# One weight remainder issued on ScalarE's queue, one small copy moved to VectorE, in the first microseconds of a fused attention and SwiGLU kernel

## The chip, the cores and the metric

The kernel runs on one core of a Trainium2 chip. The metric is device time in microseconds (us) of one execution, and a kernel's time is the median of several executions. One execution was also recorded by the hardware profiler; its rows give the start and the length of each instruction on each engine: PE (TensorE's matmuls), PEld (TensorE's weight loads), DVE (VectorE), ACT (ScalarE), POOL (GpSimd) and SP (SyncE, which here only issues DMAs). A name with a q behind it (SPq, ACTq) is the engine's instruction queue, where it issues a DMA. L145 means line 145 of the kernel file.

## The reference

One token block x of 2048 rows by 576 columns (bf16) is normalised, and two branches run on the normalised rows; their sum is added to x.

```python
xn = layernorm(x)                       # no scale, no shift
# branch A: 32 heads of 18, window of 8 keys, dilation 2, causal
q, k, v = split(xn @ wqkv)              # wqkv: 576 x 1728
o = softmax(mask(q . k[pos - 2w] * 18**-0.5), over w = 0..7) . v[pos - 2w]
# branch B: SwiGLU
h = silu(xn @ w_gate) * (xn @ w_up)     # 576 x 4608 each
out = x + o @ wo + h @ w_down           # wo: 576 x 576, w_down: 4608 x 576
```

## The kernel before

The 2048 tokens lie as 128 partitions by 16 rows: partition p holds tokens 16p to 16p+15, and "row r" is the set of 128 tokens with the same place r. The sum over the 576 columns is cut into five K tiles: four of 128, and a remainder of 64. The program is written as one straight order by hand; each engine works through its own instructions in that order, and waits are semaphores that a framework inserts. Each DMA takes the next of eight completion semaphores in turn, in program order over all queues, and waits until the DMA that had it before has landed.

The work has two stages. In the first, for each of the 16 rows, the row is normalised (VectorE, with the square root on ScalarE), turned so that K lies on partitions, and multiplied with the QKV weight on TensorE; ScalarE takes the products out of PSUM into Q, K and V. In the second stage, four groups of four rows run the SwiGLU branch in nine chunks each, with the attention of VectorE alongside, and the down and output projections at the end of each group.

The change lies in the first nine microseconds, before row 0 is multiplied. The names and lines:

- `load_x` (L145) loads one row of x for rows 0 to 3; L164 loads the other twelve in three chunks of four rows (4,608 bytes a partition).
- `load_w` (L149) loads K tile kt = 0 to 3 of the QKV weight, 128 partitions of 3,456 bytes. For kt = 4 (L152) it loads the remainder in two halves: the 64 weight rows for the first 864 output columns go to partitions 0 to 63, and the same 64 rows for the other 864 columns go to partitions 64 to 127. Each half has 64 runs of 1,728 bytes, 110.6 KB.
- The issue order before: ScalarE's queue takes row 0 of x and weight tile 1; SP's takes row 1 of x, weight tiles 0, 2, 3, the two remainder halves, rows 2 and 3 of x, and the three chunks. `load_gu` (L180 to L183) follows on SP with the first gate and up weights.
- `warm_pe` (L172, L175) keeps TensorE busy on constants until row 0 has come.
- Row 0 is treated in a way of its own: `ln_stats` (L212, L214) and `ln_sqrt` (L224, on ScalarE) work out mean and deviation; `ln_center` (L242, L244) only subtracts the mean, so that the row can be turned before the deviation is known; `transp_pe` (L250) turns it in five TensorE transposes, the first into PSUM tile `pa` and the other four into `pb`; `copy_pt` (L256) copies the turned tiles to SBUF, in three pieces: kt 0, kt 1 and 2, kt 3 and 4. The scale is applied when the products are taken out (L354, L356).
- `p_row0` calls `p_mm` (L289): for kt 0 to 3 four matmuls each, one for each group of 432 output columns; behind kt 2 the five transposes of row 1 and their copies (`first`); then four matmuls on the remainder. Groups 0 and 1 read the half on partitions 0 to 63, groups 2 and 3 the half on 64 to 127; the order is group 0, 2, 1, 3.
- Between, VectorE works on row 1 (statistics, reciprocal L229, scaling L235 and L237), whose turned form `p_row(1)` reads next.

Of the kernel before, what the change touches and what calls it, by code (L numbers as in the profile page):

```python
# [17 lines left out]
P = 128  # L18
H, DH, W, DIL = 32, 18, 8, 2
D = H * DH  # L20
HALF = D // 2
G = 432
# [48 lines left out]
def kernel(  # L71
# [11 lines left out]
    nc = tc.nc  # L83
# [6 lines left out]
    x_v = A_x.rearrange("b (p r) d -> p (b r) d", r=R)  # L90
# [33 lines left out]
    xc_b = [wdf[:, i * XC:(i + 1) * XC].rearrange("p (r d) -> p r d", d=D) for i in range(4)]  # L124
# [5 lines left out]
    wqkvr = hTf[:, 12 * D:12 * D + 2 * G]  # L130
# [13 lines left out]
    def load_x(eng, j):  # L144
        eng.dma_start(xc_b[0][:, j:j + 1, :], x_v[:, j:j + 1, :])  # L145

    def load_w(eng, kt):
        if kt < 4:
            eng.dma_start(wqkv[:, kt, :], A_wqkv[kt * P:(kt + 1) * P, :])  # L149
        else:  # L150
            for i in range(2):
                eng.dma_start(wqkvr[64 * i:64 * i + 64, :], A_wqkv[4 * P:D, 2 * G * i:2 * G * (i + 1)])  # L152

    load_x(nc.scalar, 0)
    load_x(nc.sync, 1)
    load_w(nc.scalar, 1)
    load_w(nc.sync, 0)
    make_identity(nc, ident[:])
    for kt in range(2, KT):
        load_w(nc.sync, kt)  # L160
    load_x(nc.sync, 2)
    load_x(nc.sync, 3)
    for c in range(1, 4):
        nc.sync.dma_start(xc_b[c], x_v[:, 4 * c:4 * c + 4, :])  # L164
    nc.scalar.activation(warm[:], eps_t[:], ACT.Sqrt)

    wp = ps.tile([P, 512], f32, name="warm_ps", tag="ps")
# [53 lines left out]
    def ln_sqrt(r, n=1):  # L221
        c, j = divmod(r, 4)
        xc, xn, mv, rstd = ln[c]
        nc.scalar.activation(rstd[:, j:j + n], mv[:, j:j + n, 1], ACT.Sqrt, bias=eps_t[:], scale=1.0)  # L224
# [14 lines left out]
    def ln_center(r, lo=0, hi=D):  # L239
        c, j = divmod(r, 4)  # L240
        xc, xn, mv, rstd = ln[c]
        nc.vector.tensor_scalar(xn[:, j, lo:hi], xc[:, j, lo:hi], mv[:, j, 0:1], None, op0=ALU.subtract)  # L242
        if hi == D:
            nc.vector.tensor_copy(xn[:, j, D:DPAD], xn[:, j, 512:D])  # L244

    def transp_pe(r, kts, pt):
        c, j = divmod(r, 4)
        xn = ln[c][1]
        for i, kt in enumerate(kts):
            nc.tensor.transpose(pt[:, i * P:(i + 1) * P], xn[:, j, kt * P:(kt + 1) * P], ident[:])  # L250

    def xT_of(r):
        return xcT if r == 0 else xnT[:, :, r * P:(r + 1) * P]

    def copy_pt(eng, r, kts, pt):
        eng(xT_of(r)[:, kts[0]:kts[-1] + 1, :],  # L256
            pt[:, 0:len(kts) * P].rearrange("p (k t) -> p k t", t=P))

    def new_pt():
        return ps.tile([P, 8 * P], bf16, name="pt", tag="ps")  # L260
# [213 lines left out]
    ln_stats(0)  # L474
    ln_center(0, 0, P)
    ln_sqrt(0)
    pa, pb = new_pt(), new_pt()
    transp_pe(0, (0,), pa)
    ln_center(0, P, D)
    transp_pe(0, range(1, KT), pb)  # L480
    copy_pt(nc.scalar.copy, 0, (0,), pa)
    copy_pt(nc.scalar.copy, 0, (1, 2), pb)
    ln_recip(0)
    ln_stats(1)
# [205 lines left out]
```

## Time and profile before

| | us |
|---|---|
| median of 3 runs (503.4 to 503.75) | 503.6 |
| the profiled execution, whole | 503.67 |
| its span, first to last instruction | 501.9 |
| TensorE busy in the span | 497.4 (99%) |
| VectorE busy | 329.1 (66%) |
| ScalarE busy | 200.9 (40%) |
| granted TensorE clock, mean | 1.000 |

The busy time of an engine is the time with an instruction under way, as a sum; the ends of matmuls are modelled, so a busy TensorE need not be at its peak rate. The view of the chain that ended last starts at the last instruction and goes back at each step to whatever released it; what lies on that chain sets the end, and what doesn't has slack. The timeline lists instructions by start, with the idle time of the engine before an instruction and what ended that idle time in brackets. The DMA view of a window lists packets, bytes and, by queue, the time of its packets as a share of 16 engines; q1 is the queue that SP issues on, q10 the one that ScalarE issues on.

### The profile page before, as it was taken

What the parts mean: (1) busy time and instruction counts of PE and PEld (TensorE: products, weight loads), DVE (VectorE), ACT (ScalarE), POOL (GpSimd) and SP (SyncE); (2) the same over time, 40 slices, a digit from 0 to 9 for tenths busy, and PEclk for the clock granted to TensorE, in tenths of its full rate; (3) what the DMA queues carried; (4) which work ended last, traced back from release to release, by engine and by line L of the source; (5) the groups of instructions that cost most, each with busy time, mean ns of one, the idle gap of its engine ahead of it and who ended that gap; (6) DMA issues with size and microseconds to landing.
All of it is one profiled execution on the core that took longest, in us unless ns stands there. A gap on an engine that the chain in (4) does not pass through costs nothing.

```text
span 501.9 us, 13272 instructions
## 1 busy us (share of the span) xinstructions
PE 497.4 (99%) x5799; PEld 282.9 (56%) x5799; DVE 329.1 (66%) x480; ACT 200.9 (40%) x417; POOL 0.7 (0%) x6
## 2 busy tenths in 40 slices
PE   8999999999999999999999999999999999999997
PEld 4555544444677644444777544445777444446775
DVE  5888598898999698999898139995980222221001
ACT  4756657645400255554300445557000454553000
POOL 0000000000000000000000000000000000000000
PEclk9999999999999999999999999999999999999999
DMA  8699999789922046637730154465600335552100
GB/s 311 175 192 241 305 285 315 230 266 310 232 88 61 25 133 199 185 108 226 139 103 33 29 184 141 144 188 158 136 25 14 104 105 183 149 183 39 28 14 25
DMA packets 77186, 75.42 MB, mean 150 GB/s; under 512 B 22708, under 2 KB 72528, under 8 KB 77128
## 3 DMA queue, kind: packets, MB, share of 16 engines
q1 hardware_dynamic: 76840, 73.98, 51.3%
q8 instruction: 45, 0.74, 0.6%
q10 hardware_dynamic: 288, 0.59, 0.3%
q14 instruction: 13, 0.11, 0.1%
HBM read 58.76 MB, written 5.90 MB: 129 GB/s over the span
## 4 chain that ended last, share of the span: by engine, by line
PE 98%; DMA 1%; SPq 0%; DVE 0%; issue 0%
PE g_ps L575 56%; PE d_ps L604 32%; PE qkv_ps L289 10%; DMA hT<-in_A_wqkv_dram 1%; SPq L149 0%; DVE ot L618 0%; PE pt L271 0%; SPq L145 0%
## 5 line engine op out<-in xcount | busy, mean ns | idle before, releaser
L575 PE MATMUL g_ps<-xnT,gu 64*128 64x512 bf16 x2592 | 280.4, 376 | 0.0
L575 PEld LDWEIGHTS <-gu 64*128 64x128 bf16 x2592 | 126.2, 94 | 152.9
L586 ACT ACTIVATE sg<-g_ps 128x512 bf16<-128x512 f32 x144 | 87.4, 607 | 156.6 <-PE g_ps L575 156.5
L604 PE MATMUL d_ps<-wd,hT 64*128 64x288 bf16 x2304 | 146.3, 283 | 0.0
L604 PEld LDWEIGHTS <-hT 64*128 64x128 bf16 x2304 | 112.0, 94 | 29.8
L588 DVE TENSOR_TENSOR hT<-sg,uc 128x512 bf16<-128x512 bf16 x144 | 60.2, 419 | 93.3 <-ACT uc L587 93.1
L587 ACT CAST uc<-g_ps 128x512 bf16<-128x512 f32 x144 | 85.5, 594 | 0.0
L403 DVE TENSOR_REDUCE PP<-PP 128x64 f32<-128x1152 bf16 x64 | 84.9, 1346 | 0.4
L289 PE MATMUL qkv_ps<-hT,xnT 64*128 64x432 bf16 x540 | 49.9, 342 | 0.0
L398 DVE TENSOR_TENSOR PP<-QO,Kr 128x2304 bf16<-128x2304 bf16 (+1 forms) x35 | 43.5, 1250 | 7.9 <-DMA Kr<-hT 7.6
L616 DVE TENSOR_TENSOR ot<-d_ps,xr 128x288 bf16<-128x288 f32 x30 | 12.3, 451 | 51.0 <-PE d_ps L604 51.0
L430 DVE TENSOR_TENSOR PP<-Vr,A 128x2304 bf16<-128x2304 bf16 (+1 forms) x35 | 43.3, 1251 | 0.4
L289 PEld LDWEIGHTS <-xnT 64*128 64x128 bf16 x540 | 26.1, 94 | 22.5 <-ACT xnT L275 0.2
L435 DVE TENSOR_TENSOR PP<-PP 128x2304 bf16<-128x2304 bf16 x24 | 32.5, 1354 | 0.3
L586 ACT ACT_TABLE_LOAD x5 | 6.4, 1283 | 47.2 <-PE g_ps L575 47.2
L604 PE MATMUL d_ps<-wo,xnT 64*128 64x288 bf16 x288 | 22.9, 283 | 0.0
L352 ACT CAST hT<-qkv_ps 128x288 bf16<-128x288 f32 (+2 forms) x60 | 21.9, 426 | 0.6 <-DMA Vr<-hT 0.3
L423 ACT ACTIVATE PP<-PP 128x1024 f32<-128x1024 f32 x4 | 4.2, 1056 | 31.2 <-DVE PP L419 31.2
L604 PEld LDWEIGHTS <-xnT 64*128 64x128 bf16 x288 | 14.0, 94 | 3.6
L618 ACT CAST ot<-d_ps 128x288 bf16<-128x288 f32 x1 | 0.4, 398 | 38.8 <-PE d_ps L604 38.8
L352 ACT CAST QO<-qkv_ps 128x432 bf16<-128x432 f32 (+1 forms) x30 | 12.3, 410 | 7.7 <-PE qkv_ps L289 7.7
L212 DVE BATCH_NORM_STATS2 stats<-wd 128x6 f32<-128x288 bf16 x32 | 12.9, 441 | 3.3 <-DMA wd<-in_A_x_dram 3.3
(50 smaller groups left out, 88.0 us busy)
## 6 DMA issues: line engine op xcount, KB each, us to landing
gu<-in_B_w_gate_dram SPq DMA_DIRECT2D x36, 512.0 KB, 4.0
gu<-in_B_w_up_dram SPq DMA_DIRECT2D x36, 512.0 KB, 5.3
wd<-in_B_w_down_dram SPq DMA_DIRECT2D x9, 576.0 KB, 6.3
kv_d<-hT SPq DMA_DIRECT2D x5, 576.0 KB, 5.9
gu<-in_B_w_gate_dram SPq DMA_DIRECT2D x36, 64.0 KB, 5.1
gu<-in_B_w_up_dram SPq DMA_DIRECT2D x36, 64.0 KB, 4.7
xr<-in_A_x_dram SPq DMA_DIRECT2D x8, 288.0 KB, 4.6
out_dram<-ot SPq DMA_DIRECT2D x16, 144.0 KB, 1.8
```

The costliest lines, as they stand in the source:

```text
L212: nc.vector.bn_stats(sums[r][:, k, :], xc[:, j, k * HALF:(k + 1) * HALF])
L289: return nc.tensor.matmul(t[g][:, 0:G], xT_of(r)[rows, kt, :], w_at(g, kt, rows), start=start, stop=stop)
L352: nc.scalar.copy(*parts[n])
L398: nc.vector.tensor_tensor(prod[:, a:b], QO[:, RT * tt + a:RT * tt + b, :], Kr[:, s:s + b - a, :], op=ALU.mult)
L403: nc.vector.tensor_reduce(L[:, w, rs], prod[:, rs].rearrange("p r (h d) -> p r h d", d=DH), axis=AX.X, op=ALU.add)
L430: nc.vector.tensor_tensor(dst[:, a:b], Vr[:, s:s + b - a, :].rearrange("p r (d h) -> p r d h", h=H), A[:, w, a:b].unsqueeze(2).to_broadcas ...
L435: nc.vector.tensor_tensor(dst, acc, pv, op=ALU.add)
L575: mm = nc.tensor.matmul(ring_ps[j][b][:], gu[rows, slot, k, fc], xnT[rows, kt, tok], start=(swap == 0 and kt == 0), stop=(swap == 1 and kt ...
L586: nc.scalar.activation(sg[:], t[0][:], ACT.Silu)
L587: nc.scalar.copy(uc[:], t[1][:])
L588: nc.vector.tensor_tensor(hT[:, ch * FC + j, :], sg[:], uc[:], op=ALU.mult)
L604: mm = nc.tensor.matmul(t[sub][h][:, 0:HALF], a[rows], w[rows, h * HALF:(h + 1) * HALF], start=(swap == 0 and n == 0), stop=(swap == 1 and ...
```

## The change

Two things are moved. The half of the remainder for partitions 64 to 127 is no longer issued on SP behind the first half, but on ScalarE's queue, in the program's order behind the square root of row 0. The loads of rows 2 and 3 of x and of the three chunks stay on SP in their order; in the program they now stand behind that place, so that the order in which DMAs take the eight semaphores is as before. And the copy of row 0's first turned tile (kt 0, 128 by 128) is done by VectorE instead of ScalarE; it stands on VectorE behind the 64-column copy of L244 and ahead of the reciprocal of L229. The number of instructions on TensorE and their order are as before.

```diff
@@ load_w
         else:
-            for i in range(2):
-                eng.dma_start(wqkvr[64 * i:64 * i + 64, :], A_wqkv[4 * P:D, 2 * G * i:2 * G * (i + 1)])
+            load_rem(eng, 0)
+
+    def load_rem(eng, i):
+        eng.dma_start(wqkvr[64 * i:64 * i + 64, :], A_wqkv[4 * P:D, 2 * G * i:2 * G * (i + 1)])
...
     for kt in range(2, KT):
         load_w(nc.sync, kt)
-    load_x(nc.sync, 2)
-    load_x(nc.sync, 3)
-    for c in range(1, 4):
-        nc.sync.dma_start(xc_b[c], x_v[:, 4 * c:4 * c + 4, :])
...
     ln_stats(0)
     ln_center(0, 0, P)
     ln_sqrt(0)
+    load_rem(nc.scalar, 1)
+    load_x(nc.sync, 2)
+    load_x(nc.sync, 3)
+    for c in range(1, 4):
+        nc.sync.dma_start(xc_b[c], x_v[:, 4 * c:4 * c + 4, :])
     pa, pb = new_pt(), new_pt()
     transp_pe(0, (0,), pa)
     ln_center(0, P, D)
     transp_pe(0, range(1, KT), pb)
-    copy_pt(nc.scalar.copy, 0, (0,), pa)
+    copy_pt(nc.vector.tensor_copy, 0, (0,), pa)
     copy_pt(nc.scalar.copy, 0, (1, 2), pb)
```

## The prediction

> **What bounds the kernel now.** I read three views in this order: the chain that ended last over the first 16 us, the VectorE, ScalarE and TensorE rows of the timeline around the edit, and the traffic of the DMA queues in short windows there. The chain first, cut to the stretch in question (start, length, what):
>
> ```profile
> 1.65 0.43 SPq L149
> 2.08 0.04 issue
> 2.12 6.78 DMA hT<-in_A_wqkv_dram
> 8.90 0.04 issue
> 8.94 3.73 PE qkv_ps L289 x34
> ```
>
> The end is set by one transfer: the fourth full weight tile (kt 3), issued on SP at 2.12 us, landed at 8.90. From 8.94 TensorE runs without a wait up to the tail. The windows show it: busy 18.06 of 18.06 us from 8.94 to 27, 33.00 of 33.00 up to 60, 438.00 of 438.00 up to 498. So whatever the edit does counts only by how it moves 8.94, or by a new wait behind it. All waits of TensorE in the whole span are three:
>
> ```profile
> PE warm_ps L172 <- PEq L674: 0.8, 1, 0.8
> PE pt L250 <- DVE wd L242: 0.3, 1, 0.3
> PE qkv_ps L289 <- DMA hT<-in_A_wqkv_dram: 0.2, 1, 0.2
> ```
>
> The last, 0.24 us, is the only one that a better weight stream could remove. A gain of 0.2% would be 1.0 us (about what a measurement of this kernel can tell from no change); the row bounds a gain there by 0.24.
>
> The rows around the edit (start, length, engine, line, what):
>
> ```profile
> 5.16 0.29 ACT L224 ACTIVATE rstd<-mv,eps_t 128x1 f32<-128x1 f32 x1 [2.00 <-DVE mv L214]
> 5.47 0.69 PE L250 MATMUL pt<-ident,wd 128*128 128x128 bf16 x5 [0.33 <-DVE wd L242]
> 5.70 0.18 DVE L244 COPY wd<-wd 128x64 bf16<-128x64 bf16 x1
> 5.74 0.27 ACT L256 COPY PP<-pt 128x128 bf16<-128x128 bf16 x1 [0.29 <-PE pt L250]
> 5.79 0.16 DVE L229 RECIPROCAL rstd<-rstd 128x1 f32<-128x1 f32 x1
> ...
> 6.06 2.36 PE L289 MATMUL qkv_ps<-hT,PP 128*128 128x432 bf16 x12
> 6.20 0.37 ACT L256 COPY PP<-pt 128x256 bf16<-128x256 bf16 x1 [0.20 <-PE pt L250]
> ...
> 8.26 0.44 PE L250 MATMUL pt<-ident,wd 128*128 128x128 bf16 x5
> 8.94 1.36 PE L289 MATMUL qkv_ps<-hT,PP 128*128 128x432 bf16 x8 [0.24 <-DMA hT<-in_A_wqkv_dram]
> ```
>
> The reader is to see that ScalarE copies the first turned tile at 5.74, that TensorE starts on it at 6.06, works to 8.70 and then stands still until 8.94. The matmuls on the remainder are the last four of the eight at 8.94; they start at 9.76, and the second of them, about 9.85, is the first to read partitions 64 to 127.
>
> The queues from 7.8 to 8.9 us, and then from 6.2 to 7.2 us:
>
> ```profile
> DMA packets 222, 0.25 MB, mean 228 GB/s; under 512 B 33, under 2 KB 222, under 8 KB 222
> ```
> ```profile
> DMA packets 137, 0.42 MB, mean 420 GB/s; under 512 B 15, under 2 KB 16, under 8 KB 137
> ```
>
> All engines are busy in both (104% and 103% of 16 engines). In the first no packet reaches 2 KB, so no row of a full weight tile (3,456 B) is left there; the last such packets are at 7.7, and the tile lands 1.2 us after them.
>
> **Part one: the second remainder leaves SP.** SP issued the two remainders from 2.60 to 3.94 us (0.70 and 0.60 us); they landed 6.7 and 6.3 us after issue, at 9.3 and 9.6, ahead of 9.76 and 9.85. Taking 0.60 us off SP gives nothing: SP's next issue, row 2 of x, starts at 4.05, just as the first row of x has landed (0.74 + 3.3): the program has it wait for that transfer's completion semaphore, which it takes over, and the order in which semaphores are taken over is unchanged. SP only waits longer there. The three chunks of x at 6.33 to 7.3 and the first gate and up weights at 8.92 wait for weight tiles in the same way (waits of up to 1.3 us each on the queue's own view). Sum 0.
>
> **Part two: ScalarE issues it.** It now stands behind the square root that ends at 5.45. Its price on the engine is between 0.41 us (ScalarE's own issues at 0.74 and 1.18 took 0.41 and 0.45) and 0.70 (SP's for this shape). I take 0.65, the same shape, so ScalarE is free at 6.10, and at the dear end at 6.15. Queued behind it is the copy of tiles 1 and 2, which starts at 6.20 for want of its transposes. Its reader, the fifth matmul, comes at 6.06 plus four times 0.18 (twelve in about 2.2 us), 6.78, and the copy ends at 6.57: 0.21 us more of cover. Cost 0; beyond 0.26 us of delay it would count first against the 0.24 of standstill.
>
> **Part three: the first copy moves to VectorE.** The trace has no such copy. Bounds are 0.18 us (64 columns on VectorE, L244) and 0.27 (this copy on ScalarE); the nearest row is VectorE's 256 columns from the same kind of bank, 0.24. I take 0.20. It follows the 64-column copy, where the reciprocal started at 5.79, and ends near 5.99, against 6.01 before: the first matmul moves by -0.05 to +0.1, I take 0. VectorE's later work slips by 0.17 (between 0.09, the spacing of the neighbouring rows, and 0.27): statistics and square root of row 1, its scaling, and so the five transposes at 8.26, which end at 8.87 instead of 8.70. The standstill covers that, with 0.07 left; at 0.27 it would cost 0.03. The turned row 1 is copied by 9.71 instead of 9.54, and read from 10.14. Cost 0.
>
> **Part four: the stream of weights.** The remainder's packets now come on ScalarE's queue. The first packets after x's issues at 0.74 came at 1.7 (SP) and 2.0 (ScalarE), 1.0 to 1.3 us; so here from 6.45 to 6.75, in the middle of the fourth tile, whose packets run from about 6.35 to 7.7. Before, they stood behind it. Do two queues share? Between 4.0 and 5.5 us:
>
> ```profile
> q10 hardware_dynamic: 104, 0.33, 54.3%
> q1 hardware_dynamic: 102, 0.30, 49.0%
> ```
>
> They do, packet by packet nearly equal. So the 64 packets, 110.6 KB, go between those of the fourth tile, and it ends later by at most their own service. Bounds: 0 (they come too late, or the tile's wait is in its completion and not in its packets; below nothing by 0.07, since the transposes end at 8.87) and 0.49 us (110.6 KB at the 228 GB/s of the remainders). The nearest row is the 420 GB/s of the stretch in which they arrive: 0.26. I take 0.26, since 6.75 leaves about 0.9 us of the tile's packets, and at half of 420 GB/s the 64 packets need 0.53. The first remainder lands 0.4 us behind the tile as before, at 9.56, needed at 10.0. The second lands, by the nearest row (x's first row on this queue, 3.3 us from issue to landing), at 8.75, needed at 10.1. Later work has no cost: row 2 of x, which VectorE awaited for 0.40 us at 9.94, comes no later than before.
>
> A rule speaks against any gain here: the Trainium skill, DMA: Bandwidth & Descriptors, section Issuing engines are not separate DMA queues, has all queues end on the same 16 engines, so that a second one saves only issue time; by that alone the sum would be 0, and the half shares above agree with it.
>
> **The sum.** 0 + 0 + 0 + 0.26 us on 503.67 (the profiled execution's own time; its span is 501.9, with 1.77 around it) is 503.93. That execution lies 0.07 above the median of 503.6 and inside the runs shown.
>
> **Rivals.** The second is that the fourth tile isn't pushed back, or lands earlier. For it: its 1.2 us from last packet to landing coincide with the slow stretch of the remainders, which would be shorter if both halves moved together. Against it: 0.07 us is all that the transposes leave. Time 503.60 to 503.70.
> [...]
>
> The third ends slower: the second remainder is not served beside SP's queue but behind what is in it. Place: the second matmul of the remainder, 9.85. Price: the chunk of x issued at 6.33 landed 7.3 us later; by that row the remainder lands at 5.45 + 7.3 = 12.75, TensorE stands for 2.9 us, and the time is 506.6. It decides from 4.4 us between issue and landing, and passes 0.2% at 5.4. For it: the transfers issued on SP between 1.6 and 8 us whose landing shows took 5.6 to 7.3. Against it: the equal shares from 4.0 to 5.5.
>
> The fourth: VectorE becomes the bound of the head, if the copy waits on the turned tile and pushes its chain by 0.4 us instead of 0.17. Then the transposes end at 9.10 and the time is 503.83, whatever the weights do.
>
> **How the numbers follow.** Likeliest, 0.52: the tile is pushed back by 0.1 to 0.5 us, 503.75 to 504.2. Second 0.30, third 0.08 (0.05 of it past 0.2%), fourth 0.10. The range takes in the first, second and fourth and the spread of the runs shown (0.2 below the median, 0.3 above the upper bound): 503.3 to 504.5. Faster by 0.2% has no case, since TensorE's standstill is 0.24 us: 0.02 for what I haven't seen. Slower: 0.05 and 0.01 for the same. Within: 0.92.
>
> **What would show it.** In the profile after: the chain still waits for the weight tile, now until 9.1 to 9.4, with TensorE's wait grown from 0.2 to about 0.3 to 0.4 us (the transposes end later); ScalarE's copy of tiles 1 and 2 still starts near 6.2; packets of the second queue appear between 6.4 and 7.8; no TensorE wait after that. A wait at the remainder's matmuls would be the third case, a landing at or ahead of 8.9 the second. What would make me wrong beyond the range: a late landing on ScalarE's queue, or a change of TensorE's rate after 9 us, of which the edit gives no reason.

## The result and the profile after

The changed kernel takes 506.11 us (median of six runs, 504.8 to 506.68) against 503.51 for the kernel before beside it (503.37 to 504.13): ratio 1.0045, 95% interval 1.0031 to 1.0058. Two later measurements of the same program gave 1.0025 (1.0015 to 1.0035) and 1.0023 (1.0013 to 1.0032). All three intervals lie above the 1.0005 of my forecast (503.93 to 503.67). The change makes the kernel slower, by 0.23% to 0.45%.

The profiled execution of the changed kernel took 505.31 us (span 503.5), 1.64 more than that of before. The chain that ended last, from 5.05 to 14 us (start, length, what):

```profile
5.05 5.73 DMA hT<-in_A_wqkv_dram
10.78 0.04 issue
10.83 2.76 PE qkv_ps L287 x29
13.59 0.19 PE pt L269 x6
```

The waits of its matmuls, all of them (engine, line, releaser: us in total, times, longest):

```profile
PE qkv_ps L287 <- DMA hT<-in_A_wqkv_dram: 1.0, 1, 1.0
PE warm_ps L170 <- PEq L677: 0.8, 1, 0.8
```

Before, the chain waited for the weight tile kt 3, issued at 2.12 and landed at 8.90. Now it waits for a transfer issued at 5.05: that is the moved half of the remainder, which lands 5.73 us later, at 10.78. TensorE stands for 1.0 us where there was no wait before. (Line numbers have shifted in this file: for the work of the head they are two lower, so L287 is L289 of before; for the second stage, L578 and L607 below, they are three higher.) The timeline shows where (start, length, engine, line, what, and in brackets the idle time ahead and its releaser):

```profile
3.94 0.81 SPq L145 DMA_DIRECT2D wd<-in_A_x_dram  x2
...
5.05 0.29 ACT L222 ACTIVATE rstd<-mv,eps_t 128x1 f32<-128x1 f32 x1 [1.88 <-DVE mv L212]
...
5.05 0.53 ACTq L154 DMA_DIRECT2D hT<-in_A_wqkv_dram  x1
...
5.67 0.22 DVE L254 COPY PP<-pt 128x128 bf16<-128x128 bf16 x1
...
6.09 0.37 ACT L254 COPY PP<-pt 128x256 bf16<-128x256 bf16 x1 [0.75 <-PE pt L248]
6.34 1.28 SPq L479 DMA_DIRECT2D wd<-in_A_x_dram  x3
...
8.15 0.44 PE L248 MATMUL pt<-ident,wd 128*128 128x128 bf16 x5
...
8.68 1.18 PE L287 MATMUL qkv_ps<-hT,PP 128*128 128x432 bf16 x5
...
10.83 0.52 PE L287 MATMUL qkv_ps<-hT,PP 64*128 64x432 bf16 x3 [0.97 <-DMA hT<-in_A_wqkv_dram]
```

The five matmuls at 8.68 are the four on kt 3 and the first on the remainder; the second on the remainder, the first reader of partitions 64 to 127, starts at 10.83 with 0.97 us of idle ahead. All else in these rows is on time: kt 3 was not late (8.68 against 8.94), the copies were not late.

Why does the half land so late? The queues from 5.7 to 8.4 us, and then from 8.4 to 10 us (queue: packets, MB, share of 16 engines; q10 is ScalarE's):

```profile
q1 hardware_dynamic: 452, 0.95, 104.5%
q10 hardware_dynamic: 3, 0.00, 0.1%
```

```profile
q1 hardware_dynamic: 183, 0.30, 85.9%
q10 hardware_dynamic: 79, 0.11, 27.5%
```

The half was issued at 5.05, but until 8.4 ScalarE's queue moved 3 packets and next to no bytes, while SP's moved 0.95 MB. Its data packets run from 8.57 on, half of them by 9.12, the last at 9.95. Nothing else stood in its queue. So in the main it did not go beside SP's packets; it went behind those of the transfers that SP had issued before it. The edges overlap: the last packets of the two rows of x ran until 9.44, and the first of the chunk that SP issued at 6.34 came at 9.06.

The rest of the 1.64 us comes later. For the same matmul in both traces I took the difference of the start. At 12 us TensorE is 0.97 late, at 60 us 1.01, at 490 us 1.61. Between lie short standstills, at the gate and up weights near 91 us (0.26) and at the turned attention rows near 135 us (0.34). TensorE's weight loads are counted apart from its matmuls; their waits from 80 to 140 us in the profile of after:

```profile
PEld L607 <- DMA xnT<-QO: 0.4, 1, 0.4
PEld L578 <- DMA gu<-in_B_w_gate_dram: 0.2, 1, 0.2
PEld L578 <- DMA gu<-in_B_w_up_dram: 0.2, 1, 0.2
```

Taking the three measurements of the changed program together (28 runs) its median is 505.03; all runs of the kernel before that stood beside them and the other experiments (105) have 503.68. The difference is 1.35 us.

### The profile page after: what moved, and what is told of

Its sections match the earlier page's. It is cut to its first block, busy times and chain, and to the rows that moved or that the text cites. A ratio compares the mean times of both kernels' runs of the same rounds, so it can differ in the third digit from the quotient of the medians.

```text
span 503.5 us, 13272 instructions
## 1 busy us (share of the span) xinstructions
PE 498.4 (99%) x5799; PEld 310.5 (62%) x5799; DVE 329.4 (65%) x481; ACT 200.7 (40%) x416; POOL 0.7 (0%) x6
## 4 chain that ended last, share of the span: by engine, by line
PE 95%; DMA 4%; SPq 0%; DVE 0%; issue 0%; ACT 0%
PE g_ps L578 54%; PE d_ps L607 31%; PE qkv_ps L287 10%; DMA gu<-in_B_w_up_dram 1%; DMA hT<-in_A_wqkv_dram 1%; DMA xnT<-QO 1%; DMA wd<-in_A_x_dram 1%; SPq L652 0%; DVE stats L210 0%; PE pt L269 0%; DVE ot L621 0%; SPq L178 0%; DVE mv L212 0%; SPq L636 0%; ACT rstd L222 0%
## 5 line engine op out<-in xcount | busy, mean ns | idle before, releaser
L578 PE MATMUL g_ps<-xnT,gu 64*128 64x512 bf16 x2592 | 280.8, 377 | 0.0
L578 PEld LDWEIGHTS <-gu 64*128 64x128 bf16 x2592 | 135.8, 94 | 143.6 <-DMA gu<-in_B_w_gate_dram 0.2
L607 PE MATMUL d_ps<-wd,hT 64*128 64x288 bf16 x2304 | 146.6, 283 | 0.0
L607 PEld LDWEIGHTS <-hT 64*128 64x128 bf16 x2304 | 113.6, 94 | 28.3
L287 PE MATMUL qkv_ps<-hT,xnT 64*128 64x432 bf16 x540 | 50.0, 343 | 0.0
L287 PEld LDWEIGHTS <-xnT 64*128 64x128 bf16 x540 | 42.4, 94 | 6.4 <-ACT xnT L273 0.2
L607 PE MATMUL d_ps<-wo,xnT 64*128 64x288 bf16 x288 | 22.9, 283 | 0.1
L607 PEld LDWEIGHTS <-xnT 64*128 64x128 bf16 x288 | 14.0, 94 | 3.9 <-DMA xnT<-QO 0.4
```

What stands on the lines that cost most here:

```text
L287: return nc.tensor.matmul(t[g][:, 0:G], xT_of(r)[rows, kt, :], w_at(g, kt, rows), start=start, stop=stop)
L578: mm = nc.tensor.matmul(ring_ps[j][b][:], gu[rows, slot, k, fc], xnT[rows, kt, tok], start=(swap == 0 and kt == 0), stop=(swap == 1 and kt ...
L607: mm = nc.tensor.matmul(t[sub][h][:, 0:HALF], a[rows], w[rows, h * HALF:(h + 1) * HALF], start=(swap == 0 and n == 0), stop=(swap == 1 and ...
```

## The experiments

All are compared with runs of the kernel before on the same chip. In the table, "late" is the start of the same matmul against the profile of before, at 12, 60 and 490 us of the run's own time; neighbouring matmuls scatter by up to 0.08 us around these values.

| kernel | late at 12 / 60 / 490 us | profiled run | median (range, runs) | ratio, 95% |
|---|---|---|---|---|
| after | 0.97 / 1.01 / 1.61 | 505.31 | 506.11 (504.80–506.68, 6) | 1.0045 (1.0031–1.0058) |
| e1 copy only | -0.24 / -0.24 / -0.24 | 503.50 | 503.85 (503.43–504.57, 11) | 1.0000 (0.9991–1.0008) |
| e2 DMA only | 0.87 / 0.92 / 0.93 | 504.73 | 505.75 (504.73–505.86, 5) | 1.0032 (1.0020–1.0045) |
| e3 half on SP, late | 0.60 / 0.64 / 1.46 | 505.22 | 505.22 (504.39–506.49, 11) | 1.0025 (1.0015–1.0035) |
| e4 half on ScalarE, early | 0.33 / 0.33 / 0.90 | 504.56 | 504.32 (504.14–505.38, 11) | 1.0013 (1.0004–1.0022) |
| e5 x rows behind the half | -0.11 / -0.11 / -0.11 | 504.42 | 504.68 (504.12–505.56, 11) | 1.0019 (1.0009–1.0028) |
| e6 after, again | 0.61 / 0.66 / 0.66 | 504.32 | 505.02 (504.31–506.55, 11) | 1.0025 (1.0015–1.0035) |
| e7 TensorE alone late | 0.88 / 0.94 / 0.94 | 504.57 | 504.98 (504.57–507.10, 12) | 1.0029 (1.0020–1.0038) |
| e8 chunk ahead | 1.59 / 3.29 / 3.33 | 506.98 | 506.71 (505.76–507.62, 6) | 1.0052 (1.0039–1.0065) |
| e9 before, no down weights | -0.47 / -0.47 / -0.47 | 503.30 | 503.54 (503.22–504.46, 11) | 0.9991 (0.9982–1.0000) |
| e10 after, no down weights | 1.56 / 1.62 / 1.62 | 506.15 | 505.37 (504.85–506.15, 8) | 1.0025 (1.0015–1.0035) |
| e11 after, wait filled | 0.98 / 1.02 / 1.66 | 505.33 | 505.31 (504.56–507.01, 12) | 1.0030 (1.0018–1.0042) |
| e12 after, third time | 0.94 / 0.89 / 1.37 | 505.04 | 504.89 (504.54–506.00, 11) | 1.0023 (1.0013–1.0032) |

### e1: the copy alone

```diff
--- before
-    copy_pt(nc.scalar.copy, 0, (0,), pa)
+    copy_pt(nc.vector.tensor_copy, 0, (0,), pa)
```

> The copy of row 0's first turned tile on VectorE alone; both remainder halves on SP as before. Place in line (the second half's transfer is served in order of issue over both queues, and the copy costs nothing): as before, 503.4 to 503.7 us, the weight tile kt 3 landing near 8.9 and TensorE's wait for it at 0.2 to 0.35 us. ScalarE's queue is slow by itself: the same. The copy is to blame: 504.5 or more, with a TensorE wait on VectorE.

Measured: 1.0000 (0.9991 to 1.0008). The chain:

```profile
2.12 6.53 DMA hT<-in_A_wqkv_dram
8.66 0.04 issue
8.70 3.75 PE qkv_ps L289 x34
```

It is the chain of before: weight tile kt 3 issued at 2.12, and no wait for the remainder. In this execution the tile landed at 8.66, 0.24 earlier than in the profile of before, which is all of its -0.24. The copy is worth nothing that can be measured.

### e2: the DMA alone

```diff
--- after
-    copy_pt(nc.vector.tensor_copy, 0, (0,), pa)
+    copy_pt(nc.scalar.copy, 0, (0,), pa)
```

> The second half on ScalarE behind the square root, the copy left on ScalarE behind it. Place in line: as the changed kernel, 505 to 506.5 us, the half landing near 10.8 and TensorE waiting about 1 us at the remainder's matmuls. ScalarE's queue is slow by itself: the same. The copy is to blame: 503.5 to 504.

Measured: 1.0032 (1.0020 to 1.0045). The chain has the same new member:

```profile
4.99 5.71 DMA hT<-in_A_wqkv_dram
10.69 0.04 issue
```

Issue at 4.99, landing at 10.69, TensorE 0.87 late. So the moved DMA alone brings the loss, and the copy has no part in it that shows.

### e3: the half back on SP, but at its new place in the order

```diff
--- after
-    load_rem(nc.scalar, 1)
     load_x(nc.sync, 2)
     load_x(nc.sync, 3)
+    load_rem(nc.sync, 1)
```

> Both halves on SP, but the second one issued behind rows 2 and 3 of x (near 4.5 to 5 us); copy on VectorE. Place in line: it lands behind those rows, near 10.0 to 10.8, TensorE waits 0.2 to 1.0 us at the remainder's matmuls, 504 to 506 us. ScalarE's queue is slow by itself: SP serves it as before, so 503.5.

Measured: 1.0025 (1.0015 to 1.0035). SP's queue in the timeline (the remainder's first half, rows 2 and 3 of x, the second half), and behind it the chain's entry for the half:

```profile
2.64 0.57 SPq L154 DMA_DIRECT2D hT<-in_A_wqkv_dram  x1
3.25 1.10 SPq L145 DMA_DIRECT2D wd<-in_A_x_dram  x2
4.40 0.55 SPq L154 DMA_DIRECT2D hT<-in_A_wqkv_dram  x1
```

```profile
4.40 6.02 DMA hT<-in_A_wqkv_dram
10.41 0.04 issue
```

Here no second queue is used for the half, only a place behind rows 2 and 3 of x. The half lands at 10.41, in after and its repetitions at 10.78, 10.43 and 10.71. So the queue is not what costs: the place in the order of issue is. On SP the half was even issued 0.65 us earlier than in after, and gained little from it.

### e4: the half on ScalarE's queue, early

```diff
--- after
     nc.scalar.activation(warm[:], eps_t[:], ACT.Sqrt)
+    load_rem(nc.scalar, 1)
+    load_x(nc.sync, 2)
+    load_x(nc.sync, 3)
+    for c in range(1, 4):
+        nc.sync.dma_start(xc_b[c], x_v[:, 4 * c:4 * c + 4, :])
...
     ln_sqrt(0)
-    load_rem(nc.scalar, 1)
-    load_x(nc.sync, 2)
-    load_x(nc.sync, 3)
-    for c in range(1, 4):
-        nc.sync.dma_start(xc_b[c], x_v[:, 4 * c:4 * c + 4, :])
```

> The second half on ScalarE, but issued near 3.2 us, behind the warm-up activation and ahead of the square root, so ahead of rows 2 and 3 of x; copy on VectorE. Place in line: first packets on ScalarE's queue near 7.5, behind the first half, landing near 9.5, no wait at the remainder's matmuls, 503.3 to 503.7 us. ScalarE's queue is slow by itself (3.4 us from issue to first packet): first packets near 6.6, landing at 8 to 9, and 503.5 too. Equal shares between the queues, as the prediction had it: first packets near 4.5, the tile kt 3 later by 0.26, 503.8.

Measured: 1.0013 (1.0004 to 1.0022). ScalarE in the timeline:

```profile
1.67 1.28 ACT L163 ACT_TABLE_LOAD   x1 [1.67 <-PEq L677]
1.74 0.53 ACTq L154 DMA_DIRECT2D hT<-in_A_wqkv_dram  x1
2.96 0.20 ACT L163 ACTIVATE warm<-eps_t 128x1 f32<-128x1 f32 x1
```

The issue stands behind the warm activation in the program, yet it went out at 1.74, while the activation's table was still being loaded. It thus fell between SP's issues of weight tiles 2 (1.65) and 3 (2.13). And there its packets went, from 5.51 to 7.47, ahead of the first half, which SP had issued at 2.60 and whose packets came from 7.83. The queues from 5.7 to 7.6 us:

```profile
q1 hardware_dynamic: 173, 0.54, 85.7%
q10 hardware_dynamic: 79, 0.11, 19.1%
```

Now the two queues do run in the same stretch, since their transfers were issued close together. No wait for the remainder is left. Instead kt 3, which was issued behind the half, lands at 9.23 instead of 8.90: 0.33 later, near the 0.26 that my prediction set for exactly this, the half's packets put ahead of the tile's. TensorE lost another 0.57 at a gate weight near 76 us. So the time lies above all three of the cases that I had set, none of which had so early an issue.

### e5: rows 2 and 3 of x behind the half

```diff
--- after
     load_rem(nc.scalar, 1)
-    load_x(nc.sync, 2)
-    load_x(nc.sync, 3)
+    load_x(nc.scalar, 2)
+    load_x(nc.scalar, 3)
```

> As the changed kernel (second half on ScalarE near 5.05 us), but rows 2 and 3 of x are issued on ScalarE too, right behind it, so that nothing but weights is ahead of it. ScalarE issues two DMAs more, so its copy of tiles 1 and 2 starts near 6.4 to 6.9 instead of 6.1. Place in line: the second half's first packets near 7.6 to 8 instead of 8.5, landing at 9.3 to 9.8, TensorE's wait at the remainder's matmuls 0 to 0.2 us; 503.5 to 504.3 us. ScalarE's queue is slow by itself, or its issue at 5.05 is too late whatever is ahead: first packets near 8.5 and a wait of about 1 us as in the changed kernel, 505 to 506.5.

This is the nearest to a clean test of the order: the half has the same queue and nearly the same time of issue (4.97) as in after, but rows 2 and 3 of x now follow it. The queues from 5.8 to 7.3 us, and then from 7.3 to 8.7 us:

```profile
q1 hardware_dynamic: 201, 0.62, 101.9%
q10 hardware_dynamic: 1, 0.00, 0.0%
```

```profile
q10 hardware_dynamic: 169, 0.21, 65.5%
q1 hardware_dynamic: 107, 0.17, 43.7%
```

Its packets run from 7.39 to 8.59, the middle one at 8.03 instead of 9.12, and it lands at 9.6, ahead of its reader. The two rows are 295 KB; at the 353 GB/s that the engines moved in after from 5.7 to 8.4 us they take 0.84 us, and the half's middle packet came 1.09 earlier (1.00 against e6). Until 7.3 it still waited for the tile and for the first half, both ahead of it. (SP issued the first half at 3.86 in this program, 1.26 later than in after, but its packets began at 7.11 as there, at 7.09.)

TensorE is 0.11 us ahead of before all the way, and yet the kernel is slower: 1.0019 (1.0009 to 1.0028), above the 503.5 to 504.3 that I had set. Its median lies only 0.34 us below that of the changed kernel measured beside it (e6). So that the wait is gone is shown by the profile; the times don't show that its loss is won back. In its profile the time from TensorE's last matmul to the end of the run is 5.79 us; in all others but e10 it is 4.8 to 5.0. The traffic from 498.6 to 503 us (q14 fetches instructions; the issue's last number is its time to landing):

```profile
q14 instruction: 1, 0.01, 1.1%
...
out_dram<-ot SPq DMA_DIRECT2D x1, 144.0 KB, 2.6
```

The last store of the output took 2.6 us to land; before, in after, e6, e7 and e12 it took 1.7, which is the whole difference of the tail. Here an instruction packet of 8 KB came 1.5 us after TensorE's end, beside that store. One came as early in e10, whose last store was slow too (2.2 us); in all others it came 3.5 to 4.1 us after. That the one makes the other is my reading and was not tested.

### e6 and e12: the changed kernel again

> The changed kernel again, for a second profile. It was 504.8 to 506.7 with 505.3 in the profiled execution, of which 1.0 us was at the remainder's matmuls and 0.6 in two later waits (gate and up weights at 91 us, turned attention rows at 135 us). If the later waits are made by the shift: they come again in this profile, at the same places, and the time lies 0.3 to 2 us above what the wait at the remainder explains. If they were chance: they are gone or elsewhere, and the time is 504.5.

> The changed kernel a third time, on the same chip, to compare with. 504.3 to 506.7 us, in two groups about 1.7 us apart if the clock is what divides them; its profile shows a stretch at half clock between 10 and 17 us if it lands in the upper group, and none if it lands near 504.3 to 505.3.

Measured: 1.0025 and 1.0023. The wait in e6, from the view of TensorE's waits, and the chain's entry:

```profile
PE qkv_ps L287 <- DMA hT<-in_A_wqkv_dram: 0.7, 1, 0.7
```

```profile
4.99 5.43 DMA hT<-in_A_wqkv_dram
10.43 0.04 issue
```

The half landed 0.35 us earlier than in the first profile, TensorE came 0.61 late, no later wait followed, and the run took 504.32, 0.65 more than the profile of before. In e12 the wait was 1.0 us in two pieces (0.46 for weight tile kt 3, 0.57 for the half), and at 135 us TensorE stood again for the turned attention rows; it took 505.04. So the head costs 0.6 to 1.0 us, and what comes later is not the same in each execution of one program.

### e7: TensorE late, no DMA moved

```diff
--- before
         for i in range(2):
             for half in range(2):
+                if (i, half) == (0, 1):
+                    warm_pe(5, 0)
                 p_mm(t, i + 2 * half, 4, half, 0, False, True)
```

> The kernel before, with five dummy matmuls of 512 columns ahead of the second remainder matmul (about 1.07 us of TensorE work at 0.21 us each), so that TensorE alone is late and no DMA is moved. If a shift of TensorE by 1 us brings the later waits with it: 504.9 to 506.5 us, with waits near 91 or 135 us. If a shift costs itself alone: 504.5 to 504.7, and no wait of TensorE behind 9 us.

Five matmuls on constants delay TensorE ahead of the second remainder matmul. All the waits of its matmuls are these:

```profile
PE warm_ps L172 <- PEq L676: 0.8, 1, 0.8
PE pt L250 <- DVE wd L242: 0.4, 1, 0.4
```

TensorE is 0.94 late from the head to the end, with no wait on a DMA. That profile took 0.90 us more than the one of before, but it is the fastest of its twelve runs; their median is 1.33 more than that of the kernel before beside them, as much as the changed kernel's (1.37). So a late start alone is enough for what the medians show, the part beyond the head included, though this profile doesn't show where that part arises; the transfers need not be in another order for it.

### e8: a chunk of x ahead of the half

```diff
--- after
     load_x(nc.sync, 2)
+    nc.sync.dma_start(xc_b[1], x_v[:, 4:8, :])
     load_x(nc.sync, 3)
-    for c in range(1, 4):
+    for c in range(2, 4):
         nc.sync.dma_start(xc_b[c], x_v[:, 4 * c:4 * c + 4, :])
```

> The changed kernel, but on SP the first chunk of x (590 KB) takes the place of row 3 of x (147 KB) ahead of the second half's issue near 5.0 us, so that 737 KB instead of 295 KB stand between the weights and it. Service in order of issue over both queues: 442 KB more at about 415 GB/s is 1.07 us more, the second half's packets begin near 9.6 instead of 8.6 and it lands near 11.5 to 11.9 instead of 10.4 to 10.8; TensorE's wait at the remainder's matmuls grows by 1.1 us, and the time by as much, to 505.8 to 507.5. If the lateness were fixed (ScalarE's queue, or the time of issue) the packets would begin at 8.6 again and the time be that of the changed kernel, 504.3 to 506.5.

SP issued row 2 at 3.83 and the chunk at 4.21, ahead of the half at 4.94; row 3 followed at 6.21. The chain:

```profile
4.94 6.46 DMA hT<-in_A_wqkv_dram
11.40 0.04 issue
```

737 KB stand ahead instead of 295; at the 375 GB/s that the engines moved from 5.7 to 8.4 us the 442 KB more are 1.18 us, and the middle packet came 0.86 later than in after (9.98), 0.95 later than in e6. TensorE waited 1.8 us. Then came something else; the windows from 12 us on (start and end, length, busy time and count by engine, granted clock, DMA share, GB/s):

```profile
12.00:13.00 1.00, 1.00 (x12) 0.63 (x10) 0.83 (x2) 1.00 (x5) 0.00 (x0) 0.81 1.02 410
13.00:14.00 1.00, 1.00 (x10) 0.48 (x6) 0.61 (x2) 0.44 (x2) 0.00 (x0) 0.50 0.98 387
14.00:15.00 1.00, 1.00 (x9) 0.47 (x7) 0.00 (x0) 0.00 (x0) 0.00 (x0) 0.50 1.10 367
```

The granted clock falls to 0.50, from 12.63 to 16.04 us. Half the rate over 3.41 us costs 1.70, and that is what TensorE lost between 12 and 60 us (1.59 to 3.29). It belongs to this execution: its mean granted clock is 0.996, while the other five runs have 1.000, the two slowest (507.53 and 507.62) among them. So the clock doesn't explain the median of e8.

This trace also settles whether SP's queue simply goes first. Row 3 was issued on SP at 6.21, behind the half, and its packets ran from 10.24 to 11.09; those of the half, on ScalarE's queue, from 9.11 to 10.50. So SP's later transfer did not pass it.

### e9 and e10: before and after without the down projection's weights

```diff
     make_identity(nc, ident[:])
+    u = (NF * D - 4 * XC - 2 * XN) // 2
+    nc.gpsimd.memset(wdf[:, NF * D - u:], 0.0)
+    nc.vector.memset(wdf[:, NF * D - 2 * u:NF * D - u], 0.0)
...
-                if 1 <= ch <= 7:
-                    load_wd(ch - 1)
-                if ch == 5:
-                    load_wd(8)
...
-                    load_wd(7)
```

> The kernel before without the nine loads of the down weight (5.3 MB between 60 and 130 us); that weight is left as x and zeros (two memsets at the start), so the result leaves the down projection's values out. The matmuls are all there. If the later waits come from the transfers of that stretch: the spread of the kernel before, 503.3 to 505.4, shrinks to a few tenths at its lower end, near 503.3 to 503.6. If the spread has another source: it stays.

> The changed kernel without the same nine loads, with the same values left out. The difference to the kernel before without them is the head alone if the later waits come from that stretch: 0.6 to 1.0 us, 504.1 to 504.5, with a small spread. If the later loss has another source: the difference stays at 1.3 us or more, as between the full kernels.

These were to take away the traffic with which the later waits might collide; both leave the down projection's values out of the result. The runs of e9 still spread over 1.2 us (503.22 to 504.46), beside 1.8 of the kernel before in the same measurement, so that traffic is not all that spreads them. The difference of the two medians is 1.83 us, not the 0.6 to 1.0 that I had set for a head alone. TensorE's waits for weights in e10's profile, 0.33 for tile kt 3 and 0.97 for the half:

```profile
PE qkv_ps L290 <- DMA hT<-in_A_wqkv_dram: 1.3, 2, 1.0
```

The head itself was longer there: row 0 of x landed at 4.28 instead of 3.9, so the square root and with it the half's issue came at 5.41, and it landed at 11.38. TensorE is 1.56 late in e10 and 0.47 early in e9, 2.03 apart at 12 us and 2.09 at 490 (e10's profile is also the slowest of its runs, its last store landing after 2.2 us); neither has a wait on a DMA after 12 us that moved TensorE (one weight load of e10 waited 0.2 us at 28.6). So the pair doesn't contradict that the later waits need the down weights' traffic, but with its own head it can't show it either.

### e11: the wait filled with work

```diff
--- after
             for half in range(2):
+                if (i, half) == (0, 1):
+                    warm_pe(4, 0)
                 p_mm(t, i + 2 * half, 4, half, 0, False, True)
```

> The changed kernel with four dummy matmuls (512 columns, about 0.22 us each, 0.9 us together) ahead of the second remainder matmul, so that TensorE works in most of the time in which it otherwise waits for the second half. If the runs at 506 us and more are those in which TensorE's clock was halved for 3.41 us behind the wait (1.7 us, as seen in the profile with the chunk ahead): they are gone, the upper end falls to 505.5 or so, and the median to 504.5 to 505. If they come from the transfers alone: the same spread as the changed kernel in this call, up to 506.1 to 506.7.

After e8 I suspected that the clock had also fallen in the slower runs of the changed kernel, those above 506. Here matmuls on constants fill the wait, so TensorE isn't idle. Measured: 505.31, with three of twelve runs still at 506.06 to 507.01. The upper runs are not made by the wait's idleness, and that idea falls. The clocks say the same: in none of the 28 runs of the changed kernel is the mean granted clock below 0.999, where one stretch as in e8 leaves 0.996. Its profile has a later wait of its own:

```profile
PE g_ps L580 <- DMA gu<-in_B_w_up_dram: 0.3, 1, 0.3
```

## Why the prediction was wrong

The forecast was 503.9 us, with 503.3 to 504.5 as its range; the third rival came, to which I had given 0.08.

**Part one held.** SP loses an issue and gains nothing: it issued row 2 of x at 3.94 instead of 4.05, again as row 0 landed, which came 0.11 earlier in this execution.

**Part two held in its cost.** The issue took 0.53 us, inside the bounds of 0.41 to 0.70, and ScalarE's copy started at 6.09 after 0.75 us of idle time. It was wrong about the start: I let the issue stand behind the square root's end, at 5.45; it went out at 5.05, as the square root began.

**Part three held.** The copy took 0.22 us (0.20 taken), the transposes ended at 8.59, ahead of the matmuls on the tile at 8.68. e1 confirms it: 1.0000.

**Part four failed**, at the sentence "They do, packet by packet nearly equal". I read equal shares of two queues from the stretch from 4.0 to 5.5 us. The transfers behind those packets were weight tile 1 on ScalarE's queue and, up to 5.1, tile 0 on SP's, issued at 1.18 and 1.19; then tile 2, issued at 1.65. Transfers issued so close together look the same whether queues share or whether transfers are served in the order of their issue. The row could not tell the two apart, and I used it as if it had. From it came everything else: packets from 6.45 to 6.75 (measured: from 8.57), the tile pushed back by 0.26 (measured: not at all, its last packet came at 7.64; only e4, where the half was issued ahead of the tile, has it, with 0.33), the landing at 8.75 (measured: 10.78). The price for the landing, 3.3 us, was that of a transfer issued into empty queues.

The dear bound of that part, 0.49 us, rests on a second misreading, on which the result doesn't hang. The 228 GB/s from 7.8 to 8.9 us are not the rate of the remainders: of the 189 data packets there 131 are rows of x (1,152 bytes) and 58 are of the remainders (1,728 bytes). From 8.3 to 8.9, where 105 of 117 are rows of x, the rate is still 236. So the stretch is not slow for the remainders alone. The second rival built on the same stretch. Its outcome for the tile came, with the matmuls on kt 3 starting at 8.68 instead of 8.94; but in e1, with both halves on SP, they started at 8.70, so that is not the edit's doing.

What the runs show in its place: over the two queues, the transfers of this kernel's head are served in about the order in which they were issued; neighbours in that order overlap. Moving only the two rows of x ahead of the half or behind it moves the half by 1.0 us (after, e5); the queue on which it is issued makes no difference at the same place (e3); a chunk put ahead of it delays it further (e8). Put at 1.74 us it goes at once with its contemporaries (e4). The Trainium skill, DMA: Bandwidth & Descriptors, section Queues, rings and completion order, has each engine go round robin between the queues that have work; by that, the half, alone in its queue, would have had its turn from its first packet on. The trace doesn't agree: for 3.5 us (5.05 to 8.57) it had next to none, and the measurement decides. Whether the order is kept before the engines have the packets, or in the engines, no run here tells apart.

The Trainium skill, DMA: Bandwidth & Descriptors, section Issuing engines are not separate DMA queues, on which the prediction drew, has a second queue save only time of issue. e3 agrees: on SP the half landed as late (10.41) as on ScalarE's queue (10.43 to 10.78). By the order of issue the change could only lose: it made the half's issue later (before, SP had issued both halves by 3.94), and put two rows of x ahead of it which it had stood ahead of.

**The third rival** had the mechanism and the place, the second remainder matmul. It put the decision at 4.4 us from issue to landing; measured were 5.73, and the wait was 0.97 where 5.73 less 4.4 gives 1.3 (with the issue 0.4 earlier than I had set it, 0.9). Its price of 2.9 us was too high, since I had taken it from the chunk of x. The chunk was issued at 6.33, behind the half. The row that stood nearest was row 2 of x, which VectorE awaited until 9.94 already in the kernel before; by order of issue only row 3 and the half itself follow it. An estimate from these rows, made after the result: row 3's 147 KB are 0.35 us at 420 GB/s or 0.64 at 228, and the half's own 0.26 to 0.49 are gone from ahead of row 2 and come again behind row 3, which gives 10.29 to 10.58. Or, if row 2 gains nothing from that, up to 11.07. Measured were 10.43 to 10.78.

**What stays open.** The head's delay of 0.6 to 1.0 us, with another 0.05 at the transposes of row 2, leaves 0.3 to 0.7 of the 1.35 us between the medians. In the profiles it appears as short waits for gate and up weights or for turned attention rows between 75 and 135 us, in some executions and not in others. A late TensorE alone (e7) has the same excess in its median (1.33 for 0.94), so the moved DMA is not needed for it; nor is the half clock, which no run of the changed kernel has. Whether a later start makes such waits more frequent, and why, was not found: there is one profile of most kernels. And e5 has an excess of 1.03 us in its median with no late TensorE at all, of which its profile shows 0.75, in the tail. The last store's landing, longer by 0.9 us in e5 and by 0.5 in e10, is a further place where a run can lose time that no wait of TensorE shows; how often it does so in the other runs is not known. Nor was it found why the first six runs of the changed kernel lie about 1 us above the 22 later ones.

## What to carry to other kernels

A second queue did not let a transfer overtake: here a late issue on an empty queue landed where a late issue on the busy one did. So price a moved load by the landing of those issued just ahead of and behind its new moment, on whatever queue, and keep the order of issue the order of need. And before a row is used as evidence that two things share, look whether they started together; only transfers issued at different times can show who goes first.

## What was not expected of the hardware

- A DMA issued on ScalarE's queue did not wait for the activation ahead of it in the program, from which it needed nothing: it went out at 5.05 with the square root (5.05 to 5.34), and in e4 at 1.74, 1.2 us before the activation ahead of it ran (2.96). But the copies behind it wait for the issue: in e5 two more issues moved the copy of tiles 1 and 2 from 6.09 to 6.65.
- In the profiled run of e8 a TensorE wait of 1.8 us was followed by 3.41 us at a granted clock of 0.50, for 1.7 us of loss. The five other runs of that program had the full clock, and so had the profiles with waits of 0.7 to 1.3 us in all (after, e2, e3, e6, e10, e12). The Trainium skill, TensorE: Matmul & The Clock Gate, section Part 1: The HAM clock gate, has the clock fall after an idle window of about 3.4 us. The length of the slow stretch agrees with that figure; the wait ahead of it was only half as long.
